# Packed-value products by 32-row parts of the array, into four banks, with new schedule constants

## The chip, the cores and the metric

The kernel runs on one core of a Trainium2 chip. The metric is the device time of one execution in microseconds. Before the change it is 819.77 us, the median of three runs (819.11 to 821.26). The engines are TensorE (PE in the profile; its weight loads are PEld), VectorE (DVE), ScalarE (ACT), GpSimd (POOL) and SyncE (SP), which issues the transfers.

## The reference

Eight batches, eight heads of width 64, 576 tokens. In each head 32 packing rows `p` attend over the keys and values and give 32 packed rows; then the 576 queries attend over the packed rows, which serve as keys and values both. The result, with the heads side by side (4608 tokens of 512), goes through an RMS norm and a gated MLP of inner width 1536.

```python
p_packed = sm_attn(p, k, v)              # 32 rows a head
out = sm_attn(q, p_packed, p_packed)
x = out.transpose(0, 2, 1, 3).reshape(B * S, H * D)
xn = x / rms * rms_g                      # rms = sqrt(mean(x*x) + 1e-6)
y = (silu(xn @ w_gate) * (xn @ w_val)) @ w_out
```

Outputs are float32, and the inputs `w_gate`, `w_val` and `w_out` are 64-bit numbers which the kernel turns into float32 itself.

## The kernel before

The 4608 tokens go in 12 units of 384 (three times 128 partitions). A unit is pure (its tokens are of one batch) or mixed (units 1, 4, 7 and 10: the first 64 partitions are of one batch, the other 64 of the next). Numbers are kept as a high and a low float16, so a product takes three matmuls: high by high, high by low, low by high. Units 0 and 1 compute scores in float32 instead (`early`).

Stage 1 (`stage1`, per batch) computes packing scores (L740, L749), their softmax, the transposes (L781) and the products with v (L795); the result for four heads lies on 128 partitions, 32 rows a head, in `pk`, one tile for each half of the heads. From it come `pbd` (packed rows as keys), `pg`, which `packed_weights` multiplies into the gate and value weights (L909, kept in `ring`), and `pav` (packed rows as values). The gated MLP's first product takes `ring` and the attention weights, so the attention output itself is only needed for its norm.

`attention` (per unit) multiplies the queries with `pbd` (L1048), makes a softmax and transposes the weights with a DMA (`aT`, L1088). Then it multiplies them with `pav`, squares the result and sums it: that is the attention output, and only its sum of squares for each token is used. `aT` holds on 128 partitions four heads of 32 weights each. So that one matmul serves four heads, `pav` is block-diagonal and 256 columns wide: `own` is a mask of ones in the block of each head and zeros elsewhere, and L870 multiplies it with `pk` (L875 and L877 split the result in high and low).

```python
nc.vector.scalar_tensor_tensor(pw, pks[g].unsqueeze(1).broadcast_to([P, 4, D]), sv, own, ALU.mult, ALU.mult)
```

For each third of a unit one bank (`pa`, of which there are two) takes 6 such matmuls (L1105), 12 in a mixed unit, and ScalarE squares it in place (L1110). After three of these GpSimd makes the norm (L1126 on), a one-row product (L1132) and a second transposing DMA give `aTu`. `mlp` then takes the big products: 24 groups of gate and value (L1199, four banks `pm`), activation and split (`gated`: L1233, L1236, L1241, L1247), and the output products with `w_out` (L1224).

At the start the weights come in as 1 MB pieces (`gv_piece` and `wo_piece`: L406, L411, L413), are scaled by L491, and `w_out` is summed (L523, L536, L540) and split (`wo_split`: L556, L559, L561, L567).

The order of all work on all engines is set by a planner in Python (`Plan.run`): each step is a generator that names an engine and an estimated cost, and the planner starts the step that could begin earliest, by due times (`RANK`), latencies (`LATENCY`), margins (`SLACK`, `CHOICE`) and free rooms (buffers). The estimates set only the order; on the chip each engine runs its list in order and waits on semaphores.

Of the kernel before, what the change touches and what calls it, by code (L numbers as in the profile page):

```python
# [211 lines left out]
def tile_packed_attention_then_swiglu(  # L212
# [68 lines left out]
    own = cpool.tile([P, 4, D], BF16, name="own")  # L281
    nc.gpsimd.memset(own, 0.0)
    for j in range(4):
        nc.gpsimd.memset(own[32 * j : 32 * j + 32, j, :], 1.0)

# [20 lines left out]
    rooms("pa", 2, [P, 512], F32, psum)  # L306
    rooms("psc", 1, [P, 2, 512], F32, psum)
# [410 lines left out]
    def stage1(b):  # L718
# [146 lines left out]
        for g in range(2):  # L865

            pw = yield Room("pw")
            hl = yield Room("pav")
# [1 line left out]
            nc.vector.scalar_tensor_tensor(  # L870
                pw, pks[g].unsqueeze(1).broadcast_to([P, 4, D]), sv, own, ALU.mult, ALU.mult
            )
# [148 lines left out]
    def attention(u):  # L1021
# [14 lines left out]
        yield PE, pe(64, 48) if early else len(parts(u)) * 36 * 0.03, None  # L1036
        for i in range(TPU):
            for b, r, o, n in parts(u):
                pbd = packs[b][3]
                for pi in range(4):  # L1040
                    if early:
# [4 lines left out]
                        continue  # L1046
                    for j, (lq, lp) in enumerate(((0, 0), (0, 1), (1, 0))):
                        nc.tensor.matmul(  # L1048
                            ps2[o : o + n, i, :, pi, :], qT[:, lq, i, pi, o : o + n], pbd[:, lp, pi, :, :],
                            start=(j == 0), stop=(j == 2),  # L1050
                        )
# [46 lines left out]
        for i in range(TPU):
            px = yield Room("pa")
            yield PE, pe(256, 6), t_a  # L1100
            for b, r, o, n in parts(u):
                pav = packs[b][2]
                for g in range(2):
                    for j, (la, lp) in enumerate(((0, 0), (0, 1), (1, 0))):
                        nc.tensor.matmul(  # L1105
                            px[o : o + n, 256 * g : 256 * g + 256], aT[:, i, la, g, o : o + n], pav[g][:, lp, :],
                            start=(j == 0), stop=(j == 2),
                        )
            yield ACT, act(512) + 0.2
            nc.scalar.activation(px, px, AF.Square, scale=2.0**-14, accum_out=ss[:, i : i + 1])  # L1110
            plan.give("pa", px)
# [223 lines left out]
```

## Time and profile before

| | |
|---|---|
| median of three runs | 819.77 us (819.11 to 821.26) |
| the profiled execution | 822.24 us, span 820.5 |
| TensorE busy | 762.2 us (93%), 6638 matmuls |
| VectorE busy | 496.5 us (61%) |
| ScalarE busy | 470.7 us (57%) |
| GpSimd busy | 98.0 us (12%) |
| granted TensorE clock, mean | 0.959 |
| L1105, products with packed values | 33.07 us busy, 288 matmuls |
| L1048, scores of units 2 to 11 | 14.41 us busy, 468 matmuls |

Busy time counts overlapping matmuls once, and the end of a matmul is modelled, so the length of a group is better read from the chain of waits, where each piece reaches to the start of the next. In rows of matmuls the shapes are rows x columns of the stationary weights, then output. An "x12" behind a row is the number of instructions merged in it.

### The profile page before, as it was taken

How to read it: one execution, taken by the hardware profiler on the slowest of the kernel's cores; microseconds unless marked ns; L12 is line 12 of the kernel's file. 1: busy time of each engine (PE TensorE's matmuls, PEld its weight loads, DVE VectorE, ACT ScalarE, POOL GpSimd, SP SyncE). 2: the span in 40 equal slices, each digit the busy share in tenths (PEclk: the TensorE clock that was granted, in tenths of full speed). 3: DMA queues.
4: the chain of work that ended last, by engine and by line, in shares of the span. 5: the costliest groups of instructions: out<-in, count | busy, mean ns of one | idle time of the engine just before them, and what ended most of it. 6: DMA issues, size and time to landing. Idle time of an engine off the chain costs nothing.

```text
span 820.5 us, 16153 instructions
## 1 busy us (share of the span) xinstructions
PE 762.2 (93%) x6638; PEld 445.2 (54%) x6638; DVE 496.5 (61%) x1001; ACT 470.7 (57%) x837; POOL 98.0 (12%) x149
## 2 busy tenths in 40 slices
PE   5686887989999999999979999999999999999998
PEld 4353453468555455477444556477455555576553
DVE  1797678387388367386748385566577465464341
ACT  2747887476468457467567457368566455272230
POOL 2556606100001000101010001000000001000000
PEclk9558797999999999999999999999999999999999
DMA  9991621426341940562627341725337212311001
GB/s 259 382 283 65 212 91 30 103 43 145 79 106 31 208 113 6 95 139 59 132 52 147 80 106 48 161 71 112 69 73 145 66 33 59 67 31 34 26 1 39
DMA packets 135497, 82.04 MB, mean 100 GB/s; under 512 B 98432, under 2 KB 123008, under 8 KB 135424
## 3 DMA queue, kind: packets, MB, share of 16 engines
q1 hardware_dynamic: 135424, 81.02, 41.3%
q8 instruction: 52, 0.85, 0.4%
q14 instruction: 21, 0.17, 0.1%
HBM read 47.97 MB, written 9.44 MB: 70 GB/s over the span
## 4 chain that ended last, share of the span: by engine, by line
PE 76%; DVE 9%; ACT 8%; DMA 3%; issue 2%; POOL 1%; SPq 1%; DVEq 0%; ACTq 0%; POOLq 0%
PE pm_0x L1224 9%; PE pm_1x L1224 9%; PE pm_3x L1199 8%; PE pm_2x L1224 7%; PE pm_1x L1199 7%; PE pm_2x L1199 7%; PE pm_3x L1224 7%; PE pm_0x L1199 7%; PE pm_0x L909 2%; DMA ring<-in_moe_w_gate_dram 2%; PE psc_0x L1048 2%; PE pa_0x L1105 2%; PE pa_1x L1105 2%; PE pm_2x L909 1%; DVE ring L365 1%
## 5 line engine op out<-in xcount | busy, mean ns | idle before, releaser
L1199 PEld LDWEIGHTS <-ring 128*128 128x128 f16 x2304 | 206.3, 98 | 112.4 <-issue 41.2
L1224 PEld LDWEIGHTS <-hall 128*128 128x128 f16 x1296 | 123.6, 98 | 154.9 <-issue 16.5
L1224 PE MATMUL pm_1x<-wo,hall 128*128 128x512 f16 x360 | 83.2, 381 | 5.6 <-POOL wo L567 3.1
L1224 PE MATMUL pm_0x<-wo,hall 128*128 128x512 f16 x360 | 82.4, 379 | 0.0
L1224 PE MATMUL pm_2x<-wo,hall 128*128 128x512 f16 x324 | 72.6, 379 | 0.0
L1241 ACT CAST hall<-t_1x 128x384 f16<-128x384 f32 x72 | 36.7, 510 | 43.4 <-DVE t_1x L1236 42.8
L1224 PE MATMUL pm_3x<-wo,hall 128*128 128x512 f16 x252 | 56.9, 379 | 0.0
L1199 PE MATMUL pm_3x<-aTu_1x,ring 128*128 128x192 f16 (+1 forms) x372 | 50.8, 281 | 1.6 <-ACT t_1x L1233 1.1
L1241 ACT CAST hall<-t_0x 128x384 f16<-128x384 f32 x72 | 36.6, 509 | 26.6 <-DVE t_0x L1236 25.9
L1247 DVE TENSOR_TENSOR hall<-t_1x,hall 128x384 f16<-128x384 f32 x72 | 40.0, 556 | 18.1 <-ACT hall L1241 16.7
L1247 DVE TENSOR_TENSOR hall<-t_0x,hall 128x384 f16<-128x384 f32 x72 | 41.1, 571 | 13.7 <-ACT hall L1241 13.4
L1199 PE MATMUL pm_3x<-aTu_0x,ring 128*128 128x384 f16 (+1 forms) x300 | 45.3, 294 | 0.4 <-ACT t_1x L1233 0.2
L1199 PE MATMUL pm_1x<-aTu_0x,ring 128*128 128x192 f16 (+1 forms) x306 | 42.4, 282 | 1.4 <-DVE tiny_30x L775 1.3
L1199 PE MATMUL pm_2x<-aTu_0x,ring 128*128 128x192 f16 (+1 forms) x306 | 42.4, 282 | 0.0
L1199 PE MATMUL pm_2x<-aTu_1x,ring 128*128 128x384 f16 (+1 forms) x246 | 38.1, 297 | 3.6 <-DVE ring L365 2.6
L1199 PE MATMUL pm_1x<-aTu_1x,ring 128*128 128x384 f16 (+1 forms) x276 | 40.1, 288 | 0.1
L1199 PE MATMUL pm_0x<-aTu_1x,ring 128*128 128x192 f16 (+1 forms) x258 | 38.4, 295 | 1.2 <-ACT t_1x L1233 1.1
L1199 PE MATMUL pm_0x<-aTu_0x,ring 128*128 128x384 f16 (+1 forms) x240 | 35.5, 290 | 0.0
L1105 PEld LDWEIGHTS <-aT_0x 128*128 128x128 f16 (+1 forms) x288 | 23.7, 104 | 9.4 <-issue 5.8
L1233 ACT ACT_TABLE_LOAD x15 | 19.2, 1283 | 7.4 <-PE pm_1x L1199 2.8
L363 ACT ACTIVATE ring<-pm_2x,pw_sc 128x512 f16<-128x512 f32 x27 | 18.4, 683 | 6.9 <-PE pm_3x L909 4.7
L365 DVE SCALAR_TENSOR_TENSOR ring<-pm_0x,pw_sc,ring 128x512 f16<-128x512 f32 x26 | 19.4, 745 | 4.4 <-ACT ring L363 3.9
(848 smaller groups left out, 1312.6 us busy)
## 6 DMA issues: line engine op xcount, KB each, us to landing
out_dram<-o_1x SPq DMA_DIRECT2D x18, 256.0 KB, 2.2
out_dram<-o_0x SPq DMA_DIRECT2D x18, 256.0 KB, 2.0
wo<-in_moe_w_gate_dram SPq DMA_DIRECT2D x3, 1024.0 KB, 15.3
wo<-in_moe_w_val_dram SPq DMA_DIRECT2D x3, 1024.0 KB, 13.7
ring<-in_moe_w_out_dram SPq DMA_DIRECT2D x3, 1024.0 KB, 6.0
hall<-in_moe_w_out_dram SPq DMA_DIRECT2D x3, 1024.0 KB, 5.4
big_0x<-in_k_dram SPq DMA_DIRECT2D x5, 576.0 KB, 6.9
big_2x<-in_k_dram SPq DMA_DIRECT2D x5, 576.0 KB, 6.2
```

Source lines behind the costliest of these rows:

```text
L363: nc.scalar.activation(hi, x, AF.Copy, scale=s)
L365: nc.vector.scalar_tensor_tensor(lo, x, s, hi, ALU.mult, ALU.subtract)
L909: nc.tensor.matmul(ps[e][32 * j : 32 * j + 32, :], pg[h, j, :], wgv[h, c, j, :, :].rearrange("p w f -> p (w f)"), start=True, stop=True,)
L1048: nc.tensor.matmul(ps2[o : o + n, i, :, pi, :], qT[:, lq, i, pi, o : o + n], pbd[:, lp, pi, :, :], start=(j == 0), stop=(j == 2),)
L1105: nc.tensor.matmul(px[o : o + n, 256 * g : 256 * g + 256], aT[:, i, la, g, o : o + n], pav[g][:, lp, :], start=(j == 0), stop=(j == 2),)
L1199: nc.tensor.matmul(psi[:, :, o : o + n], pw[:, g, lw, w, f * P : (f + 1) * P], aT[:, :, la, g, o : o + n], start=(j == 0), stop=(j == 5),)
L1224: nc.tensor.matmul(po, hall[:, ft, lh, ts], wo[:, ft, lw, :], start=(n == 0), stop=(n == 3 * NFT - 1))
L1233: nc.scalar.activation(t, pss[0][:, :UT], AF.Silu, scale=sc[:, c, 0:1])
L1241: nc.scalar.copy(hall[:, ft, 0, :], t)
L1247: nc.vector.tensor_tensor(hall[:, ft, 1, :], t, hall[:, ft, 0, :], ALU.subtract)
```

## The change

- `pav` is no longer block-diagonal. It keeps the 32 rows of each head where they lie on the partitions, 64 columns wide, and is split straight from `pk` by the helper `split` (in the profile its lines are those of L363 and L365). `own`, `pw` and L870 to L877 are gone.
- A matmul of the packed values now takes 32 rows of the array (one head, `tile_position=(32 * j, o)`) and 64 columns of output. The four heads j write into four different banks. A pure unit has 72 such matmuls (3 thirds x 2 halves x 3 terms x 4 heads) where it had 18, a mixed one 144 where it had 36, each with its own weight load.
- The four banks are one tile `quad`; its first two are the old `psc` and the other two the old `pa`. The block of a whole unit takes all four at once, then come the three squares, each over 128 columns of each bank, then the banks are given back.
- In the scores of a mixed unit (L1048) the two batches' matmuls alternate (they use different columns of the array), where before the first batch's twelve came ahead of the second's.
- `LATENCY`, `SLACK`, `CHOICE` and `RANK` get other values, and the two steps other estimated costs; with them the planner sets another order.

```diff
-LATENCY = {PE: 0.25, ACT: 0.16, EXP: 0.16, SILU: 0.16, DVE: 0.14, POOL: 0.1}
-SLACK = (0.3, 0.3)
-CHOICE = {"pe": 0.0, "act": 0.3, "dve": 0.3, "pool": 0.5, "sp": 0.3}
+LATENCY = {PE: 0.293, ACT: 0.16, EXP: 0.16, SILU: 0.16, DVE: 0.14, POOL: 0.1}
+SLACK = (0.306, 0.3)
+CHOICE = {'pe': 0.1, 'act': 0.335, 'dve': 0.324, 'pool': 0.378, 'sp': 0.437}
...
-    "scales": 0.1, "gated": 0.2, "pw_evict": 0.3, "store": 0.4, "attention": 0.5, "stage1": 0.6, "keys": 0.65, "v": 0.66,
-    "query": 0.7, "pw": 0.8, "g": 0.9, "w": 1.0, "wo": 1.5, "wo_split": 1.8,
+RANK = {"scales": 0.1, "gated": 0.44, "pw_evict": 0.3, "store": 0.4, "attention": 0.63, "stage1": 0.6, "keys": 0.67, "v": 0.66, "query": 0.79, "pw": 0.8, "g": 0.9, "w": 1.0, "wo": 1.5, "wo_split": 1.65}
...
-    rooms("pa", 2, [P, 512], F32, psum)
-    rooms("psc", 1, [P, 2, 512], F32, psum)
+    quad = psum.tile([P, 4, 512], F32, name="quad")
+    plan.rooms["psc"] = [(0.0, quad[:, 0:2])]
+    plan.rooms["pa"] = [(0.0, quad[:, 2]), (0.0, quad[:, 3])]
...
-            nc.vector.scalar_tensor_tensor(
-                pw, pks[g].unsqueeze(1).broadcast_to([P, 4, D]), sv, own, ALU.mult, ALU.mult
-            )
+            yield from split(hl[:, 0], hl[:, 1], pks[g], sv, D, t_s)
             plan.give("pk", pks[g])
-            yield ACT, act(256)
-            nc.scalar.copy(hl[:, 0], pw.rearrange("p h d -> p (h d)"))
-            yield DVE, dve(256) + 0.1
-            nc.vector.tensor_tensor(hl[:, 1], pw.rearrange("p h d -> p (h d)"), hl[:, 0], ALU.subtract)
...
-        yield PE, pe(64, 48) if early else len(parts(u)) * 36 * 0.03, None
+        yield PE, pe(64, 48) if early else 36 * 0.03 + 0.1 * len(parts(u)), None
         for i in range(TPU):
-            for b, r, o, n in parts(u):
-                pbd = packs[b][3]
-                for pi in range(4):
+            for pi in range(4):
...
-                    for j, (lq, lp) in enumerate(((0, 0), (0, 1), (1, 0))):
+                for j, (lq, lp) in enumerate(((0, 0), (0, 1), (1, 0))):
+                    for b, r, o, n in parts(u):
                         nc.tensor.matmul(
...
-        for i in range(TPU):
-            px = yield Room("pa")
-            yield PE, pe(256, 6), t_a
-            for b, r, o, n in parts(u):
-                pav = packs[b][2]
-                for g in range(2):
-                    for j, (la, lp) in enumerate(((0, 0), (0, 1), (1, 0))):
-                        nc.tensor.matmul(
-                            px[o : o + n, 256 * g : 256 * g + 256], aT[:, i, la, g, o : o + n], pav[g][:, lp, :],
-                            start=(j == 0), stop=(j == 2),
-                        )
-            yield ACT, act(512) + 0.2
-            nc.scalar.activation(px, px, AF.Square, scale=2.0**-14, accum_out=ss[:, i : i + 1])
-            plan.give("pa", px)
+        held = [("psc", (yield Room("psc")))]
+        for _ in range(2):
+            held.append(("pa", (yield Room("pa"))))
+        px = quad[:, :, : TPU * 2 * D].rearrange("s j (i g d) -> s j i g d", i=TPU, g=2)
+        yield PE, pe(D, 6 * TPU) + 0.4, t_a
+        for i in range(TPU):
+            for g in range(2):
+                for n3, (la, lp) in enumerate(((0, 0), (0, 1), (1, 0))):
+                    for j in range(4):
+                        h = slice(32 * j, 32 * j + 32)
+                        for b, r, o, n in parts(u):
+                            nc.tensor.matmul(
+                                px[o : o + n, j, i, g, :], aT[h, i, la, g, o : o + n], packs[b][2][g][h, lp, :],
+                                start=(n3 == 0), stop=(n3 == 2), tile_position=(32 * j, o),
+                            )
+        t = plan.now
+        for i in range(TPU):
+            yield ACT, act(512) + 0.2, t
+            x = px[:, :, i].rearrange("s j g d -> s j (g d)")
+            nc.scalar.activation(x, x, AF.Square, scale=2.0**-14, accum_out=ss[:, i : i + 1])
+        for name, room in held:
+            plan.give(name, room)
```

The order moves on every engine. Three places are shown; in the changed kernel the line numbers are smaller (L1099 is the old L1105, L1197 the old L1199, L898 the old L909, L793 the old L795, L747 the old L749).

First, TensorE in unit 4's big products, around the packed-value products of unit 5. Before, from stage 1's value products on (weight loads and equal rows in between are left out):

```order
L795 MATMUL pa_1x<-big_2x,a1T_0x 32x64 x24
...
L1199 MATMUL pm_3x<-aTu_0x,ring 128x3x64
...
L1105 MATMUL pa_0x<-pav_2x,aT_0x 128x256
...
L1105 MATMUL pa_0x<-pav_3x,aT_0x 128x256
...
L749 MATMUL psc_0x<-big_5x,pT_0x 32x288
...
L1105 MATMUL pa_1x<-pav_2x,aT_0x 128x256
...
L1132 MATMUL pa_1x<-ru_1x,onesb 128x3
```

And in the changed kernel:

```order
L793 MATMUL quad<-big_2x,a1T_0x 32x64 x24
...
L1197 MATMUL pm_2x<-aTu_0x,ring 128x3x64
...
L1099 MATMUL quad<-pav_2x,aT_0x 128x64
...
L1099 MATMUL quad<-pav_3x,aT_0x 128x64
...
L898 MATMUL pm_1x<-wgv,pg_1x 32x512
...
L747 MATMUL quad<-big_5x,pT_0x 32x288
...
L1130 MATMUL quad<-ru_1x,onesb 128x3
```

The three pieces, which lay apart and on both sides of stage 1's scores, are one block now, 24 big products behind stage 1's value products and, with a packing pair and 36 big products between, ahead of its next scores. The products of unit 4 itself stand, in the changed kernel, two packing pairs and 54 big products behind that unit's scores (before: one pair, 96 big products and 39 output products).

Second, SyncE's transfers at the start. Before:

```order
L578 DMA big_0x<-in_k_dram 96x4x384
L578 DMA big_2x<-in_k_dram 96x4x384
L601 DMA pf_0x<-in_p_dram 32x2x64 x4
L578 DMA big_1x<-in_v_dram 96x4x384
L970 DMA wgv<-in_q_dram 128x8x192
L376 DMA o_0x<-in_moe_rms_g_dram 128x512
L444 DMA ring<-in_moe_w_gate_dram 128x4x512
L578 DMA big_3x<-in_v_dram 96x4x384
L378 DMA gcol<-in_moe_rms_g_dram 128x4x1
L444 DMA ring<-in_moe_w_val_dram 128x4x512
```

And in the changed kernel:

```order
L576 DMA big_0x<-in_v_dram 96x4x384
L576 DMA big_2x<-in_v_dram 96x4x384
L576 DMA big_1x<-in_k_dram 96x4x384
L576 DMA big_3x<-in_k_dram 96x4x384
L599 DMA pf_0x<-in_p_dram 32x2x64 x4
L959 DMA wgv<-in_q_dram 128x8x192
L374 DMA o_0x<-in_moe_rms_g_dram 128x512
L442 DMA ring<-in_moe_w_gate_dram 128x4x512
L376 DMA gcol<-in_moe_rms_g_dram 128x4x1
L442 DMA ring<-in_moe_w_val_dram 128x4x512
```

Both halves of batch 0's v went ahead of its keys; from the second piece of the weights on the same bytes are ahead as before.

Third, ScalarE late in unit 0's gate products, from the last sum of w_out's squares (L523, now L521) to the first casts of the split (L561, now L559). Before:

```order
L523 ACTIVATE o_0x,wo_ss<-wo_83 128x1024
L786 COPY a1T_0x<-psc_0x 96x768
L1233 ACT_TABLE_LOAD
L1233 ACTIVATE t_0x<-pm_1x,usc_0x 128x384
L1233 ACTIVATE t_1x<-pm_2x,usc_0x 128x384
L556 ACTIVATE big_2x<-wo_83,wo_sc 128x1024
...
L556 ACTIVATE big_5x<-wo_83,wo_sc 128x1024
L999 ACTIVATE big_3x,tiny_46x<-big_0x 128x8x3x64
L833 ACTIVATE pts_0x<-pa_0x,tiny_50x 128x128
L561 CAST wo_83<-big_2x 128x2x512
```

And in the changed kernel:

```order
L521 ACTIVATE o_0x,wo_ss<-wo_77 128x1024
L1231 ACT_TABLE_LOAD
L1231 ACTIVATE t_1x<-pm_3x,usc_0x 128x384
L1231 ACTIVATE t_0x<-pm_2x,usc_0x 128x384
...
L554 ACTIVATE big_0x<-wo_77,wo_sc 128x1024
...
L831 ACTIVATE pts_0x<-quad,tiny_47x 128x128
L554 ACTIVATE big_4x<-wo_77,wo_sc 128x1024
...
L559 CAST wo_77<-big_0x 128x2x512
```

The sum came forward from behind ten of the unit's twelve activations to behind seven, the square of the next query (L999) and three of its splits (L363) fell behind the last cast, and the casts of `pav` (L875) became the narrow L363 of `split`. On TensorE the product L540, which closes the sum, stands behind 108 of unit 0's 144 gate products instead of all of them.

More of the change, by code (lines that the diff above doesn't have):

```diff
@@ L50, in pe @@
     return count * max(n / 2400 + 0.0025, 0.029)
+ACT_COST = (0.076, 0.87e-3)
+DVE_COST = (0.08, 1.04e-3)
 def act(n):
-    return 0.1 + 0.87e-3 * n
+    return ACT_COST[0] + ACT_COST[1] * n
 def dve(n):
-    return 0.08 + 1.04e-3 * n
+    return DVE_COST[0] + DVE_COST[1] * n
 def pool(n):
@@ L279, in tile_packed_attention_then_swiglu @@
     nc.gpsimd.memset(qk1, QK)
[L281 to L284, printed above, removed]
     wgv = cpool.tile([P, NFC, NKT, 2, 2 * P], F32, name="wgv")
@@ L322, in tile_packed_attention_then_swiglu @@
     rooms("pg", 2, [P, 4, NPK], F32)
-    rooms("pw", 1, [P, 4, D], F32)
-    rooms("pav", 4, [P, 2, 4 * D], F16)
+    rooms("pav", 4, [P, 2, D], F16)
     rooms("junk", 2, [P, D], BF16)
@@ L1035, in attention @@
         ps2 = psx.rearrange("s (i e j r) -> s i e j r", i=TPU, e=2, j=4)
-        yield PE, pe(64, 48) if early else len(parts(u)) * 36 * 0.03, None
+        yield PE, pe(64, 48) if early else 36 * 0.03 + 0.1 * len(parts(u)), None
         for i in range(TPU):
-            for b, r, o, n in parts(u):
-                pbd = packs[b][3]
-                for pi in range(4):
-                    if early:
+            for pi in range(4):
+                if early:
+                    for b, r, o, n in parts(u):
                         nc.tensor.matmul(
@@ L1045, in attention @@
                         )
-                        continue
-                    for j, (lq, lp) in enumerate(((0, 0), (0, 1), (1, 0))):
+                    continue
+                for j, (lq, lp) in enumerate(((0, 0), (0, 1), (1, 0))):
+                    for b, r, o, n in parts(u):
                         nc.tensor.matmul(
-                            ps2[o : o + n, i, :, pi, :], qT[:, lq, i, pi, o : o + n], pbd[:, lp, pi, :, :],
+                            ps2[o : o + n, i, :, pi, :], qT[:, lq, i, pi, o : o + n], packs[b][3][:, lp, pi, :, :],
                             start=(j == 0), stop=(j == 2),
@@ L1097, in attention @@
         t_x = []
[L1098 to L1111 removed]
+        held = [("psc", (yield Room("psc")))]
[3 more added lines that the diff above has]
+        yield PE, pe(D, 6 * TPU) + 0.4, t_a
+        for i in range(TPU):
+            for g in range(2):
+                for n3, (la, lp) in enumerate(((0, 0), (0, 1), (1, 0))):
+                    for j in range(4):
+                        h = slice(32 * j, 32 * j + 32)
+                        for b, r, o, n in parts(u):
+                            nc.tensor.matmul(
[7 more added lines that the diff above has]
+            nc.scalar.activation(x, x, AF.Square, scale=2.0**-14, accum_out=ss[:, i : i + 1])
             t_x.append(plan.now)
+        for name, room in held:
+            plan.give(name, room)
         plan.give("aT", aT)
```

5 lines of the change are left out of this document (removed).

## The prediction

> **What bounds the kernel now.** I read the page first (span, busy shares, the row of slices), then the busy time in five stretches, then the chain that ended last.
>
> ```profile
> span 820.5 us, 16153 instructions
> PE 762.2 (93%) x6638; PEld 445.2 (54%) x6638; DVE 496.5 (61%) x1001; ACT 470.7 (57%) x837; POOL 98.0 (12%) x149
> core 0: us, PE busy (x) PEld busy (x) DVE busy (x) ACT busy (x) POOL busy (x), PEclk, DMA share, GB/s
> 0.00:90.00 90.00, 58.70 (x523) 37.33 (x523) 57.68 (x111) 50.63 (x76) 47.90 (x65) 0.74 0.81 243
> 90.00:120.00 30.00, 29.18 (x280) 17.52 (x272) 22.01 (x45) 27.32 (x49) 6.16 (x9) 0.97 0.49 155
> 120.00:160.00 40.00, 30.35 (x209) 15.22 (x210) 27.39 (x48) 26.00 (x43) 15.98 (x12) 0.87 0.27 62
> 160.00:750.00 590.00, 577.53 (x5294) 341.72 (x5293) 370.80 (x769) 354.74 (x648) 27.92 (x64) 0.99 0.41 87
> PE 76%; DVE 9%; ACT 8%; DMA 3%; issue 2%; POOL 1%; SPq 1%; DVEq 0%; ACTq 0%; POOLq 0%
> ```
>
> From 160 to 750 us TensorE is busy for 577.5 of 590 us at a granted clock of 0.99; VectorE has 371 us of work there (63%), ScalarE 355 (60%). After 750 us only products are left. So whatever leaves TensorE's queue after 160 us shortens the run almost one for one, until the 12.5 us of idle time grow. Before 160 us it is different: the DMA share is 0.81 up to 90 us, ScalarE has 27.3 of 30 us from 90 to 120 us, and TensorE idles 9.7 us from 120 to 160 us. The profiled execution took 822.24 us (1.7 outside its span) and the median of the runs shown is 819.77; I make the sum against the former and take 2.5 us off for the latter.
>
> **Products with packed values, as they are.** From the chain in order of time, one piece for a pure unit (one batch), then for a mixed one (two batches), with the score products L1048 of both kinds:
>
> ```profile
> 190.05 0.66 PE pa_1x L1105 x6
> 331.40 1.02 PE pa_0x L1105 x12
> 333.82 1.02 PE pa_1x L1105 x12
> 168.00 1.05 PE psc_0x L1048 x36
> 302.88 1.90 PE psc_0x L1048 x72
> 304.77 1.08 PE pm_1x L1199 x6
> 307.95 0.97 PE pm_1x L1199 x6
> 357.26 1.10 PE pm_2x L1199 x12
> 90.28 1.73 PE pm_3x L1199 x6
> ```
>
> Each unit has three pieces: 1.98 us in a pure unit, 3.06 in a mixed one. Seven pure units (2, 3, 5, 6, 8, 9, 11) and four mixed ones (1, 4, 7, 10) run after 150 us, 26.1 us in all. Unit 0 lies before 90 us, where TensorE has room, and I count it as nothing; if that room were gone it would be worth the 1.1 us that a pure unit saves below. The rows of L1199 give the pace of the big products around (six in 0.97 to 1.08 us in a pure unit, twelve in 1.10 in a mixed one) and the first of them, at 90.3 us.
>
> **What they become.** 72 matmuls of 32 rows x 64 columns in a pure unit and 144 in a mixed one, each with its own weight load. The arithmetic in rows of the array is a quarter; the time depends on whether four row parts (times two column parts in a mixed unit) run at once. No such matmul is in the trace. Its nearest relatives are the packing products (64 rows x 32 columns, eight parts, timeline of TensorE) and the stage-1 products (four column parts, first and last start of 48):
>
> ```profile
> 301.79 0.61 PE L909 MATMUL pm_0x<-wgv,pg_1x 64*32 64x512 f32 x1
> ...
> 301.83 0.61 PE L909 MATMUL pm_2x<-wgv,pg_1x 64*32 64x512 f32 x1
> 302.24 0.59 PE L909 MATMUL pm_0x<-wgv,pg_1x 64*32 64x512 f32 x1
> ...
> 302.81 0.38 PE L1048 MATMUL psc_0x<-pbd,big_1x 128*64 128x64 f16 x6
> L795 PE MATMUL pa_0x<-big_5x,a1T_0x x48: 219/219/243, 118.3 to 118.9; 96*32 96x64 f32 x48
> ```
>
> Eight packing products start within 0.04 to 0.05 us, some 6.5 ns apart, and all eight of the next round 0.45 us later: parts with different rows and columns do run together. Two rounds take 1.02 us up to the next line, of which 0.90 is streaming, so a block of another tiling costs about 0.12 us for going in and out. The 48 stage-1 products follow each other at 0.6/47 = 13 ns, the fastest pace that is shown over a long run.
>
> - Low end: 18 rounds. A round takes the larger of one 64-column product (1.05/36 = 29 ns) and its issue at 6.5 ns each (26 ns for four, 52 for eight). Pure 18 x 29 + 0.12 us = 0.65 us, mixed 18 x 52 + 0.12 us = 1.06 us.
> - High end, still overlapping: 13 ns for each instruction. Pure 72 x 13 + 0.12 us = 1.06 us, mixed 144 x 13 + 0.12 us = 1.99 us.
> - No overlap at all is a rival below.
>
> The packing products are nearer in kind (row parts), the stage-1 products in length of the run, so I take the middle: 0.86 and 1.53 us. Saved: 7 x 1.12 = 7.8 and 4 x 1.53 = 6.1 us; ends 6.4 to 9.3 and 4.3 to 8.0.
>
> **Score products of mixed units.** The two batches write different column halves of the array; in turn instead of one after the other they should pair, so that 72 cost what 36 of a pure unit cost, 1.05 us, instead of 1.90. Three units (4, 7, 10): 2.6 us; nothing if column parts don't pair, which the 13 ns above speak against. The fp32 products of unit 1 are interleaved too, in a stretch where TensorE idles, so I count nothing. Sum on TensorE: 16.5 us.
>
> **Around the block.** Four banks are held at once, and the three squares follow the whole block instead of a third of it.
>
> ```profile
> L1110 ACT ACTIVATE pa_0x<-pa_0x x19: 577/582/607, 67.8 to 729.3; 128x512 f32<-128x512 f32 x19
> L1110 ACT ACTIVATION_READ_ACCUMULATOR pa_0x<-pa_0x x19: 181/194/202, 68.3 to 729.8; 128x1 f32 x19
> PE pa_0x L1105 <- ACT pa_0x L1110: 0.2, 1, 0.2
> 476.00 1.97 PE L1048 MATMUL psc_0x<-pbd,big_1x 128*64 128x64 f16 x72
> ...
> 486.71 1.44 SPq L1088 DMA_TRANSPOSE aT_0x<-hl_0x  x1
> DMA to landing us min/median/max: 3.6/3.7/4.4
> ```
>
> The squares are as many and as long: 3 x (0.58 + 0.19) = 2.3 us a unit, on an engine with 40% to spare. From the end of the scores (302.88 + 1.90 gives their length; here 476.0 + 1.9 = 477.9) to the landing of aT (486.7 + 3.7 = 490.4) it is 12.5 us. In the new order unit 4 has two packing pairs and 54 products of L1199 between scores and block, 2 x 1.02 + 9 x 0.97 = 10.8 us: 1.7 us short. The other units have 12 us or more by the same count. I put down 2 us lost, between 0 and 4. Behind the waiting matmul stands the whole of TensorE.
>
> **Packed values.** Each batch loses two wide VectorE products and their casts:
>
> ```profile
> L870 DVE SCALAR_TENSOR_TENSOR pw_0x<-pk_2x,tiny_50x,own x1: 2350/2350/2350, 131.4 to 131.4; 128x256 f32<-128x256 f32 x1
> L870 DVE SCALAR_TENSOR_TENSOR pw_0x<-pk_0x,tiny_80x,own x1: 484/484/484, 225.3 to 225.3; 128x256 f32<-128x256 f32 x1
> ```
>
> Later, at 0.48 us, that hides under TensorE's 98% and is worth nothing (if VectorE became the bound, about 1 us a batch). At 131 us, where TensorE waits, it counts in the next part.
>
> **Start.** Here the constants move things.
>
> ```profile
> GB/s 259 382 283 65 212 91 30 103 43 145 79 106 31 208 113 6 95 139 59 132 52 147 80 106 48 161 71 112 69 73 145 66 33 59 67 31 34 26 1 39
> big_0x<-in_k_dram SPq DMA_DIRECT2D x5, 576.0 KB, 6.9
> PE pm_1x L1224 <- POOL wo L567: 3.1, 2, 1.6
> PE pm_1x L1224 <- ACT wo L561: 2.5, 1, 2.5
> PE pa_1x L819 <- ACT junk_1x L807: 3.0, 1, 3.0
> L999 ACT ACTIVATE big_5x<-big_2x 128x1536 bf16<-128x1536 f32 x2 | 3.0, 1481 | 1.6 <-DMA big_2x<-in_q_dram 1.6
> L363 ACT ACTIVATE ring<-pm_2x,pw_sc 128x512 f16<-128x512 f32 x27 | 18.4, 683 | 6.9 <-PE pm_3x L909 4.7 <-PE pm_0x L909 1.9 <-PE pm_1x L909 0.3
> ```
>
> Against: SP now loads both halves of v ahead of k. At the 382 GB/s of the second slice a half of 576 KB is 1.5 us, so k, the first products behind it and SP's queue start up to 3 us later; the weights move back by 1.5 us at first and not at all from the second piece on, since the same bytes are then ahead. For: ScalarE reaches the last cast of w_out (L561) with one L999 (1.5 us) and three L363 of the next query (3 x 0.68) less ahead of it and one ring eviction more, some 2.9 us less, and the sum of w_out's squares stands 36 products of L1199 earlier on TensorE. The 8.6 us of waits quoted are what this can reach. I take 2 us gained, between 6 gained and 4 lost.
>
> **Sum.** 16.5 - 2 + 2 = 16.5 us: 822.24 becomes 805.7 for a profiled run, and 819.77 becomes 803.3 for the median, about 803. With all ends together, 19.9 + 6 = 25.9 gained gives 794, and 13.3 - 4 - 4 = 5.3 gained gives 814.5.
>
> **Rivals.**
>
> 1. The parts don't overlap: one instruction in a row costs what L1048 shows, 29 ns at 128 columns and 1.90/72 = 26.4 ns at 64. Pure 72 x 29.2 + 0.12 us = 2.22 us (+0.24), mixed 144 x 26.4 + 0.12 us = 3.92 us (+0.86), the scores stay: 1.7 + 3.4 us lost, start and late aT cancel, 819.8 + 5.1 = 825. For it: in L1048 every 64-column product costs its whole 26 to 29 ns. Against it: L909's 6.5 ns. [...] Chance 0.08.
>
> 2. Only column parts overlap. Pure as in 1 (+1.7 us), mixed 144 x 13.2 + 0.12 us = 2.02 us (4 x 1.04 saved), scores 2.6 saved: 5.1 us gained, 815. L795 shows column parts alone; row parts are shown with 64 rows only. Chance 0.12.
>
> 3. The late k and the new order of w_out's work cost 6 us instead of gaining 2: 803.3 + 8 = 811. ScalarE's 27.3 of 30 us speak for it, the equal amount of DMA against it. Chance 0.12.
>
> 4. Slower: the block needs all four banks free, and holds them until ScalarE has squared them. In units 5 and 8 stage 1's value products end 24 products (2.2 us) ahead of the block and its next scores come 36 products and a packing pair (4.3 us) behind it; if VectorE's read or the 2.3 us of squares queue behind the activation of the gate, TensorE stops. It decides from 16.5/11 = 1.5 us a unit on; at 2.5 us a unit the time is 803.3 + 27.5 = 831. For it: the old kernel could use three rooms in turn. Against: its wait for a bank is 0.2 us in the whole run, and ScalarE and VectorE idle for 40%. Chance 0.08.
>
> **Chances and range.** Forecast 0.6, rivals 0.08, 0.12, 0.12, 0.08. A measurement of this kernel tells about 0.3% (2.5 us) from no change, so faster is below 817.3: the forecast, rivals 2 and 3, 0.84. Rival 1 lies at the edge of the other side; I give 0.06 to no change and 0.10 to slower. The range goes from 793 to 816: the forecast's ends and rivals 2 and 3.
>
> **What would show it.** In the new timeline, four starts of the block's matmuls within some 30 ns, a pure block of 0.65 to 1.06 us, a mixed one of 1.06 to 1.99, mixed scores near 1.05. Waits for aT at unit 4 of 1 to 2 us. TensorE idle from 160 us on no more than some 14 us. Scores or stage-1 products waiting for a square (L1110's successor) over 1.5 us a unit would make rival 4; a pure block above 2 us makes rival 1 or 2; a first product of L1199 later than 93 us makes rival 3 (it now starts at 90.3).

## The result, and the profile after

The changed kernel takes 797.96 us (median; 796.5 to 799.99), the kernel before 820.0 us in the same comparison (819.11 to 821.26): a ratio of 0.973, with an interval from 0.971 to 0.976. The profiled executions took 796.5 and 822.24 us, spans of 794.5 and 820.5.

First the chain of waits of the changed kernel (start, length, engine, group, count): a pure block, then scores and block of a mixed unit, then the block of the next mixed unit.

```profile
178.07 0.68 PE quad L1099 x72
...
293.81 1.26 PE quad L1037 x72
309.15 1.30 PE quad L1099 x144
...
475.85 1.43 PE quad L1099 x144
```

A pure block takes 0.68 us (0.69 and 0.75 in two units) where three pieces took 1.98, a mixed one 1.30 to 1.43 (1.49 in unit 1) where they took 3.06, and the mixed scores 1.26 where they took 1.90.

Next the stretch that the sum was about. It is cut here at the first big product of unit 1 and at the last matmul, so that it holds the same products before and after, except for unit 2's pure scores (1.05 us), which the changed kernel has already done. The columns are length, then busy time and count of TensorE, weight loads, VectorE, ScalarE and GpSimd, then the granted clock, the DMA share and GB/s. Before, then after:

```profile
166.80:816.50 649.70, 637.19 (x5599) 371.50 (x5597) 385.71 (x791) 363.00 (x666) 27.31 (x62) 0.99 0.37 81
```

```profile
166.10:790.80 624.70, 617.59 (x6265) 356.53 (x6263) 375.86 (x774) 364.37 (x668) 27.90 (x62) 1.00 0.38 84
```

TensorE is busy 19.6 us less and idle 7.1 us instead of 12.5. The clock rises from 0.99 to 1.00, and that small step matters. Here is the kernel before around its wait in unit 1, from the timeline and then in stretches of 1 us:

```profile
183.04 1.46 PE L1199 MATMUL pm_2x<-aTu_1x,ring 128*128 128x192 f16 x12 [2.64 <-DVE ring L365]
184.56 2.08 PE L1199 MATMUL pm_0x<-aTu_1x,ring 128*128 128x192 f16 x12
```

```profile
182.00:183.00 1.00, 0.00 (x0) 0.00 (x0) 1.00 (x3) 1.00 (x2) 0.00 (x0) 1.00 0.00 0
183.00:184.00 1.00, 0.96 (x11) 0.94 (x11) 1.00 (x2) 0.98 (x2) 0.00 (x0) 0.87 0.00 0
184.00:185.00 1.00, 0.94 (x8) 0.68 (x6) 1.00 (x2) 0.99 (x2) 0.00 (x0) 0.50 0.06 16
185.00:186.00 1.00, 1.00 (x9) 0.92 (x7) 0.96 (x2) 0.73 (x3) 0.00 (x0) 0.50 0.96 182
186.00:187.00 1.00, 1.00 (x9) 0.92 (x7) 0.25 (x1) 0.51 (x1) 0.00 (x0) 0.50 1.11 198
187.00:188.00 1.00, 1.00 (x18) 0.83 (x24) 0.89 (x3) 0.53 (x2) 0.00 (x0) 0.93 0.99 152
```

After a wait of 2.64 us the clock is granted at 0.50 for some 3.4 us, and the twelve products that start at 184.56 take 1.88 us up to the next twelve, instead of 1.10. That is 3.4 x 0.5 = 1.7 us lost beyond the wait. The kernel before has two such drops from 160 us on (the other behind two waits close together, of 2.8 and 1.1 us), the changed kernel none. The waits of that time, before and after (engine, group, what it waited for, us in total, times, longest):

```profile
PE pa_0x L1132 <- POOL ru_0x L1128: 2.8, 1, 2.8
PE pm_2x L1199 <- DVE ring L365: 2.6, 1, 2.6
PE pm_3x L1199 <- ACT t_1x L1233: 1.3, 2, 1.1
PE pm_1x L1199 <- DVE tiny_30x L775: 1.3, 1, 1.3
```

```profile
PE pm_3x L1197 <- DVE ring L363: 1.7, 1, 1.7
PE pm_3x L1197 <- ACT t_1x L1231: 1.0, 1, 1.0
PE quad L747 <- ACT quad L1107: 0.7, 1, 0.7
...
PE quad L1099 <- DMA aT_0x<-hl_0x: 0.3, 1, 0.3
```

So the 26.0 us between the spans come apart as follows: idle time 12.5 - 7.1 = 5.4; two clock drops 3.4; work on TensorE 15.1 (the difference of the busy time, 19.6, less the drops, less the 1.05 us of scores that moved ahead of the cut); the lead at the cut 0.7 + 1.05 = 1.8; and 0.3 behind the last matmul. I had forecast 15.0 us of work behind the cut (16.5 with unit 1's block, which lies ahead of it), and nothing for the idle time and the clock. Added up from the pieces of the chain, the blocks and scores behind the cut save 16 us; where the other 0.9 us of the busy time went, no run shows.

### The profile page after: what moved, and what is told of

Its sections match the earlier page's. It is cut to its first block, busy times and chain, and to the rows that moved or that the text cites. A ratio compares the mean times of both kernels' runs of the same rounds, so it can differ in the third digit from the quotient of the medians.

```text
span 794.5 us, 17852 instructions
## 1 busy us (share of the span) xinstructions
PE 737.0 (93%) x7502; PEld 425.1 (54%) x7502; DVE 483.9 (61%) x985; ACT 472.2 (59%) x839; POOL 101.4 (13%) x144
## 4 chain that ended last, share of the span: by engine, by line
PE 78%; ACT 7%; DVE 6%; DMA 5%; SPq 2%; issue 2%; POOL 1%; ACTq 0%; DVEq 0%; POOLq 0%
PE pm_2x L1222 11%; PE pm_1x L1222 10%; PE pm_2x L1197 8%; PE pm_1x L1197 8%; PE pm_0x L1222 8%; PE pm_3x L1197 7%; PE pm_0x L1197 7%; PE pm_3x L1222 6%; DMA hall<-in_moe_w_gate_dram 2%; PE pm_3x L898 2%; SPq L442 2%; PE quad L1037 1%; DMA big_3x<-in_k_dram 1%; PE pm_0x L898 1%; PE quad L793 1%
## 5 line engine op out<-in xcount | busy, mean ns | idle before, releaser
L1197 PEld LDWEIGHTS <-ring 128*128 128x128 f16 x2304 | 205.7, 98 | 107.0 <-issue 35.9
L1222 PE MATMUL pm_2x<-wo,hall 128*128 128x512 f16 x396 | 90.1, 379 | 0.0
L1239 ACT CAST hall<-t_1x 128x384 f16<-128x384 f32 x72 | 36.8, 510 | 34.9 <-DVE t_1x L1234 34.3
L1245 DVE TENSOR_TENSOR hall<-t_1x,hall 128x384 f16<-128x384 f32 x72 | 41.7, 579 | 17.2 <-ACT hall L1239 14.8
L1245 DVE TENSOR_TENSOR hall<-t_0x,hall 128x384 f16<-128x384 f32 x72 | 41.6, 578 | 14.9 <-ACT hall L1239 14.6
L1222 PE MATMUL pm_3x<-wo,hall 128*128 128x512 f16 x216 | 49.2, 383 | 0.0
L1197 PE MATMUL pm_2x<-aTu_0x,ring 128*128 128x192 f16 (+1 forms) x324 | 45.6, 285 | 1.0 <-DVE ring L363 0.6
L1197 PE MATMUL pm_1x<-aTu_1x,ring 128*128 128x192 f16 (+1 forms) x324 | 45.8, 285 | 0.2 <-ACT t_0x L1231 0.2
L1197 PE MATMUL pm_3x<-aTu_1x,ring 128*128 128x192 f16 (+1 forms) x288 | 41.2, 286 | 3.1 <-DVE ring L363 1.7
L1197 PE MATMUL pm_1x<-aTu_0x,ring 128*128 128x192 f16 (+1 forms) x312 | 43.5, 283 | 0.2 <-ACT t_0x L1231 0.2
L1197 PE MATMUL pm_2x<-aTu_1x,ring 128*128 128x192 f16 (+1 forms) x288 | 41.3, 286 | 0.9 <-ACT hall L1239 0.7
L1197 PE MATMUL pm_0x<-aTu_0x,ring 128*128 128x384 f16 (+1 forms) x270 | 40.2, 291 | 0.7 <-ACT t_1x L1231 0.3
L1197 PE MATMUL pm_3x<-aTu_0x,ring 128*128 128x384 f16 (+1 forms) x246 | 37.6, 296 | 0.6 <-ACT t_1x L1231 0.5
L1197 PE MATMUL pm_0x<-aTu_1x,ring 128*128 128x384 f16 (+1 forms) x252 | 36.6, 288 | 0.0
L363 DVE SCALAR_TENSOR_TENSOR ring<-pm_3x,pw_sc,ring 128x512 f16<-128x512 f32 x31 | 23.1, 745 | 9.1 <-ACT ring L361 9.0
L361 ACT ACTIVATE ring<-pm_3x,pw_sc 128x512 f16<-128x512 f32 x31 | 21.1, 682 | 7.3 <-PE pm_0x L898 5.7
L1107 ACT ACTIVATE quad<-quad 128x512 f32<-128x512 f32 x36 | 21.1, 587 | 6.7 <-PE quad L1099 6.2
L363 DVE SCALAR_TENSOR_TENSOR ring<-pm_0x,pw_sc,ring 128x512 f16<-128x512 f32 x27 | 20.1, 746 | 7.8 <-ACT ring L361 7.4
## 6 DMA issues: line engine op xcount, KB each, us to landing
wo<-in_moe_w_val_dram SPq DMA_DIRECT2D x3, 1024.0 KB, 10.8
```

Of the source, the lines that this page charges most:

```text
L361: nc.scalar.activation(hi, x, AF.Copy, scale=s)
L363: nc.vector.scalar_tensor_tensor(lo, x, s, hi, ALU.mult, ALU.subtract)
L1107: nc.scalar.activation(x, x, AF.Square, scale=2.0**-14, accum_out=ss[:, i : i + 1])
L1197: nc.tensor.matmul(psi[:, :, o : o + n], pw[:, g, lw, w, f * P : (f + 1) * P], aT[:, :, la, g, o : o + n], start=(j == 0), stop=(j == 5),)
L1222: nc.tensor.matmul(po, hall[:, ft, lh, ts], wo[:, ft, lw, :], start=(n == 0), stop=(n == 3 * NFT - 1))
L1239: nc.scalar.copy(hall[:, ft, 0, :], t)
```

## Experiments: what a block costs

All comparisons are with the kernel before, timed on the same chip (820.4 to 820.7 us).

**Heads in turn.** The head j becomes the outermost loop, so that neighbouring matmuls of a batch use the same 32 rows. The order of everything else stays.

```diff
+        for j in range(4):
+            h = slice(32 * j, 32 * j + 32)
-        for i in range(TPU):
-            for g in range(2):
-                for n3, (la, lp) in enumerate(((0, 0), (0, 1), (1, 0))):
-                    for j in range(4):
-                        h = slice(32 * j, 32 * j + 32)
+            for i in range(TPU):
+                for g in range(2):
+                    for n3, (la, lp) in enumerate(((0, 0), (0, 1), (1, 0))):
```

> The changed kernel with the four heads outermost in the block: the same 72 or 144 matmuls, banks and squares, but 18 in a row use the same 32 rows of the array. Theory A (the gain is that neighbours use different row parts and run at once): a pure block takes 72 x 29 ns = 2.1 us instead of 0.68, a mixed one about half of 144 x 29 ns = 2.1 instead of 1.3 to 1.5; 7 x 1.4 + 4 x 0.7 = 12.6 us more, 811. Rival (short matmuls with a quarter of the rows are quick in any order): blocks as they are, 798.

Measured: 809.09 us, ratio 0.985 (0.982 to 0.987), 11.1 us above the changed kernel. From its chain, and its stretch from unit 1 on:

```profile
180.68 1.90 PE quad L1099 x72
...
314.53 2.10 PE quad L1099 x141
```

```profile
168.70:803.70 635.00, 628.32 (x6265) 367.52 (x6263) 375.72 (x774) 365.56 (x668) 27.99 (x62) 1.00 0.37 83
```

72 matmuls through the same rows take 1.90 us, 26.4 ns each; spread over four row parts they take 0.68, 9.4 ns each. So the row parts do run at once, and that is where the gain of a pure block lies. In a mixed unit the two column parts alone bring it to 2.10/144 = 14.6 ns. Whether the 26.4 ns are a cost of each matmul or the time of its columns, no run here shows: the big products take 0.97 us for six times 384 columns, 0.42 ns a column, so that 64 columns streamed one matmul after the other would take 27 ns as well (an estimate from these rows). The 9.4 ns show that across row parts this time is not paid by each matmul in turn.

This run also measures what TensorE's time is worth when the order is fixed: 7 x 1.22 us in pure blocks and 0.80 + 0.67 + 0.80 in mixed ones make 10.8 us, the busy time grows by 10.7 and the stretch by 10.3. One for one.

**Half the columns.** Each of the block's matmuls writes 32 columns, and the squares read only these; half of each head's attention output is left out of the norm.

```diff
-    px[o : o + n, j, i, g, :], aT[h, i, la, g, o : o + n], packs[b][2][g][h, lp, :],
+    px[o : o + n, j, i, g, : D // 2], aT[h, i, la, g, o : o + n], packs[b][2][g][h, lp, : D // 2],
...
-            x = px[:, :, i].rearrange("s j g d -> s j (g d)")
+            x = px[:, :, i, :, : D // 2]
```

> The block's matmuls write 32 columns of output where they wrote 64, and the squares read those alone: half of each head's attention output is left out of the norm. The order and the number of instructions stay. Theory A (a block is limited by issue, about 9 ns for a matmul with its weight load): a pure block stays at 0.65 to 0.70 us. Rival B (limited by the columns streamed through each row part): a pure block of 0.35 to 0.45 us. Total within 2 us of 798 by A, 3 to 5 us less by B; the squares are half as long (on ScalarE, with room).

Measured: 795.86 us in a single run, 2.1 us below the changed kernel's median but 0.6 below its profiled execution. The timeline of the same pure block, in the changed kernel and here:

```profile
178.01 0.27 PE L1099 MATMUL quad<-pav_2x,aT_0x 32*128 32x64 f16 x12
...
178.47 0.28 PE L1099 MATMUL quad<-pav_3x,aT_0x 32*128 32x64 f16 x12
178.68 0.61 PE L898 MATMUL pm_0x<-wgv,pg_1x 64*32 64x512 f32 x1
```

```profile
179.06 0.24 PE L1099 MATMUL quad<-pav_2x,aT_0x 32*128 32x32 f16 x12
...
179.51 0.27 PE L1099 MATMUL quad<-pav_3x,aT_0x 32*128 32x32 f16 x12
179.71 0.61 PE L898 MATMUL pm_0x<-wgv,pg_1x 64*32 64x512 f32 x1
```

The block shrinks from 0.67 to 0.65 us although half the columns are gone; 60 of the 72 matmuls start within 0.46 and 0.45 us. So here not the streaming but the number of matmuls, some 8 ns for one with its weight load, sets the length; whether the matmul or its load sets the pace, no run separates. One rival comes close in a pure block: a fixed 26.4 ns in each row part, shared by four parts, would give 6.6 ns. The mixed block speaks against it: there eight parts run, and a matmul still takes 1.30/144 = 9.0 ns.

**Scores apart.** In mixed units the two batches' scores follow each other again, as before the change.

```diff
-            for pi in range(4):
...
-                for j, (lq, lp) in enumerate(((0, 0), (0, 1), (1, 0))):
-                    for b, r, o, n in parts(u):
+            for b, r, o, n in parts(u):
+                for pi in range(4):
+                    for j, (lq, lp) in enumerate(((0, 0), (0, 1), (1, 0))):
```

> The changed kernel, but in the scores of mixed units the first batch's twelve matmuls come ahead of the second's again; everything else stands in the same order. Theory A: each of the three mixed score groups goes from 1.26 back to 1.90 us on a TensorE without room, 798 + 1.9 = 800. Rival: the time is taken up by a later wait, 798.

Measured: 800.07 us, ratio 0.975 (0.974 to 0.977), 2.1 us above the changed kernel. Its chain, the same wait in its timeline as the changed kernel's 1.7 us on `ring`, and the clock behind it:

```profile
293.47 1.90 PE quad L1038 x72
```

```profile
303.23 1.41 PE L1198 MATMUL pm_3x<-aTu_1x,ring 128*128 128x384 f16 x6 [2.02 <-DVE ring L363]
```

```profile
304.00:305.00 1.00, 1.00 (x5) 0.46 (x3) 1.00 (x2) 0.99 (x2) 0.00 (x0) 0.50 0.00 0
```

The scores are back at 1.90 us, 3 x 0.64 = 1.9 us in all, close to the difference of the medians. The profiled execution shows something beside it: the wait is 0.36 us longer, and a clock drop of 1.7 us follows it. Its span is 2.8 us longer than the changed kernel's, with a start of unit 1 that is 0.7 us earlier. How much of the medians' difference is scores and how much is clock is therefore not shown.

## Experiments: what the order costs

The planner's numbers were part of the change: LATENCY, SLACK, CHOICE, RANK, and its estimate of a ScalarE step (0.1 us + 0.87 ns an element before, 0.076 us + 0.87 ns now). The estimate stands in the planner's cost functions, and the account of the change above leaves it out; the first two runs left it as the kernel they started from had it. In all these kernels the instructions of the products are those of the kernel named; only the numbers, and with them the order, differ. In the expectations "theory A" means what each text says there, not one theory throughout.

**The changed kernel with the old four, and the kernel before with the new four.**

```diff
-LATENCY = {PE: 0.293, ...}; SLACK = (0.306, 0.3); CHOICE = {'pe': 0.1, ...}; RANK = {..., "gated": 0.44, ...}
+LATENCY = {PE: 0.25, ...};  SLACK = (0.3, 0.3);   CHOICE = {"pe": 0.0, ...}; RANK = {..., "gated": 0.2, ...}
```

> The changed kernel with the old LATENCY, SLACK, CHOICE and RANK: new products, order made by the old constants. Theory A (the gain is TensorE's time in the two groups of products, 15.5 us in the packed-value products and 2.0 in the mixed scores, and the other 4.5 us of the 22 are waits that the new order avoids): 800.5 to 804, about 802.5, the blocks still 0.68 us (pure) and 1.3 to 1.5 (mixed). Rival B (most of the gain comes from the order that the constants make): 810 or more. If the constants are worth nothing: 798.

> The kernel before with the new LATENCY, SLACK, CHOICE and RANK: old products, order made by the new constants. Theory A: 4.5 us of waits avoided, 813 to 818, about 815.5. Rival B: 808 or less. Rival C (the constants fit the new products alone): 820 or more.

Measured: 815.86 us (ratio 0.995, 0.993 to 0.996) and 835.75 us (1.018, 1.016 to 1.020). My theory, that the constants are worth a few us by themselves (800.5 to 804 and 813 to 818), fell on both sides: the new products alone gained 4.6 us, the new four constants alone lost 15.3, both together gained 22. Since the estimate had stayed behind, the next two runs moved all five.

**All five old with the new products, all five new with the old products, and the estimate alone, in each kernel.**

```diff
-ACT_COST = (0.076, 0.87e-3)
+ACT_COST = (0.1, 0.87e-3)
```

This is the estimate going back in the changed kernel; in the kernel before it goes the other way, and the two runs with all five have the four of above with it.

> The new products with every planner constant of before; the estimated cost of a ScalarE step (0.1 us + 0.87 ns an element, where the change and the earlier run with old constants had 0.076) goes back too. Theory A (new products in an order that is not fitted to them keep their saving on TensorE and give most of it back as waits): within 4 us of that earlier run's 815.9, so 812 to 820, with TensorE idle 10 us or more from 160 to 750 us beyond the 7.1 us of the changed kernel. Rival B (the mixture of old constants with the new ScalarE cost was what failed; a consistent old set carries the products' 16 us): 806 or less.

> The old products with every new planner constant, the ScalarE cost of 0.076 us among them. Theory A (the new constants fit the new products alone): 825 to 840, near the 835.8 without that cost. Rival B (only the missing ScalarE cost made that run slow, the new constants are better by themselves): 815 or less.

> The changed kernel with one number back: the planner's estimate of a ScalarE step, 0.1 instead of 0.076 us. Theory A (any number reorders the whole list, and an order is good or bad as a whole): 803 to 816, the time lost is TensorE's idle time from 160 us on, the blocks stay at 0.68 and 1.31 to 1.50 us. Rival B (the order is worth little, time follows TensorE's work): within 2 us of 798.

```diff
-    return 0.1 + 0.87e-3 * n
+    return 0.076 + 0.87e-3 * n
```

> The kernel before with the planner's estimate of a ScalarE step at 0.076 instead of 0.1 us, nothing else. Theory A (any number reorders the whole list; the old order was one of the better ones for the old products): 820 to 836. Rival B (this estimate is the better one, whatever the products): 817 or less.

Measured: 812.98 us (ratio 0.991, 0.990 to 0.993), 821.11 (1.001, 0.999 to 1.002), 801.49 (0.977, 0.975 to 0.978) and 828.66 (1.010, 1.007 to 1.012). So with all five moved the new constants do nothing for the old products, and "they fit the new products alone and harm the old ones" (825 to 840) fell too, as did its rival (815 or less). The estimate alone in the changed kernel came out between theory A (803 to 816) and its rival (within 2 us of 798); the other two lie in theory A's ranges. One estimate, changed by 0.024 us, costs 3.5 us in the changed kernel and 8 us in the one before.

**RANK alone, and LATENCY, SLACK and CHOICE alone, back in the changed kernel.**

```diff
-RANK = {..., "gated": 0.44, ..., "attention": 0.63, ..., "keys": 0.67, ..., "query": 0.79, ..., "wo_split": 1.65}
+RANK = {..., "gated": 0.2, ..., "attention": 0.5, ..., "keys": 0.65, ..., "query": 0.7, ..., "wo_split": 1.8}
```

> The changed kernel with the old RANK (the due times) alone; the other constants stay new. Theory A (each set of numbers is another whole order, none of the constants has a price of its own): 801 to 813, and TensorE's waits from 160 us on rise by about what the time rises. Rival B (RANK carries the fit): 810 or more, near the 813.0 with all constants old, and then the run with the other constants old is within 2 us of 798.

```diff
-LATENCY = {PE: 0.293, ...}; SLACK = (0.306, 0.3); CHOICE = {'pe': 0.1, 'act': 0.335, 'dve': 0.324, 'pool': 0.378, 'sp': 0.437}
+LATENCY = {PE: 0.25, ...};  SLACK = (0.3, 0.3);   CHOICE = {"pe": 0.0, "act": 0.3, "dve": 0.3, "pool": 0.5, "sp": 0.3}
```

> The changed kernel with the old LATENCY, SLACK and CHOICE; RANK stays new. Theory A: 801 to 813, as for the old RANK alone. Rival B (RANK carries the fit): within 2 us of 798. Rival C (these three carry it): 810 or more.

Measured: 808.5 us (ratio 0.984, 0.983 to 0.986) and 816.36 (0.995, 0.993 to 0.996). RANK back costs 10.5 us, the three others 18.4, all five together only 15.0. RANK lies in theory A's range, though TensorE's idle time rises by 4.2 us only (table below); the three others lie above that range, where rival C had them. The parts don't add up; no constant has a price of its own.

**k first.** The first load of v gets a later due time, so that SP loads k and p ahead of v, as before the change.

```diff
-    plan.add(load_v(0), due("v", 0))
+    plan.add(load_v(0), due("v", 0) + 2.0)
```

> The changed kernel with the first load of v due later, so that k and p go first at the start, as before the change. TensorE's first wait, for p, falls from 13.8 to about 9.4 us. Theory A (the start up to 90 us is set by the weights' transfers and by ScalarE, and the early products have room): the first big product still starts at 84 to 86 us, and the time is 798 to 806, as this number too reorders the list. Rival B (the 4.4 us at the start are on the path): 793 to 796.

Measured: 800.27 us, ratio 0.975 (0.974 to 0.977), 2.3 us slower. From its waits:

```profile
PE pm_0x L610 <- DMA pf_0x<-in_p_dram: 8.7, 1, 8.7
PE quad L793 <- DMA big_4x<-in_v_dram: 6.0, 1, 6.0
```

TensorE's first wait falls from 13.8 to 8.7 us, and 6.0 us of wait for v come in its place. The first big product starts at 88.2 us instead of 84.8. So the time lies in theory A's range, the start (84 to 86 us) does not. From unit 1 on the run is the changed kernel's again (624.6 and 624.7 us).

**All orders in one table.** The stretch from unit 1's first big product to the last matmul, in us, ordered by time. "Lost to clock" is the sum over stretches of 0.25 us of TensorE's busy time x (1 - granted clock); "idle" is length less busy time, so a drop during a wait counts once, as idle time.

| kernel | time | unit 1 starts | busy | of it lost to clock | idle |
|---|---|---|---|---|---|
| old products, own constants (before) | 820.6 | 166.8 | 637.2 | 3.4 | 12.5 |
| old products, all five new | 821.1 | 167.7 | 635.0 | 3.0 | 12.4 |
| old products, estimate new | 828.7 | 169.2 | 636.2 | 3.2 | 15.2 |
| old products, four new | 835.8 | 169.8 | 637.7 | 3.4 | 23.8 |
| new products, own constants (after) | 798.0 | 166.1 | 617.6 | 0 | 7.1 |
| new products, k first | 800.3 | 169.6 | 617.7 | 0 | 6.9 |
| new products, estimate old | 801.5 | 163.9 | 617.9 | 0 | 14.9 |
| new products, RANK old | 808.5 | 171.8 | 621.7 | 2.9 | 11.3 |
| new products, all five old | 813.0 | 161.7 | 626.8 | 7.8 | 18.6 |
| new products, four old | 815.9 | 166.3 | 625.1 | 4.6 | 18.7 |
| new products, three old | 816.4 | 166.8 | 622.5 | 3.2 | 21.6 |

Busy time without the clock's loss is 632.1 to 634.3 us with the old products and 617.6 to 620.5 with the new ones. Counting unit 2's scores alike (they lie ahead of the cut in all but the kernel before and the runs with all five and with three old), the means are 634.1 and 619.4, and the orders of either kernel lie within 3 us: the products are worth 14.6 us of TensorE's work in all eleven orders. What an order adds in this stretch is 7 to 24 us of idle time and 0 to 8 us of clock, and that decides what a single swap seems to show. The four sets of constants that were run with both products give 7.6, 12.8, 34.3 and 23.1 us for the products, 19 in the mean.

The clearest case is the new products with all five old constants, so the plain exchange of the products under the old numbers. Its stretch, the longest waits in it, and the clock around the first of them:

```profile
161.70:807.10 645.40, 626.84 (x6301) 362.77 (x6299) 376.65 (x778) 362.49 (x667) 28.03 (x62) 0.98 0.37 82
```

```profile
PE pm_0x L1200 <- DMA aTu_0x<-hl_0x: 4.3, 1, 4.3
PE pm_0x L1200 <- DVE ring L366: 3.2, 2, 2.6
PE pm_2x L1200 <- DVE ring L366: 3.0, 2, 2.8
PE quad L700 <- ACT big_4x L694: 2.6, 1, 2.6
```

```profile
343.00:344.00 1.00, 0.00 (x0) 0.00 (x0) 0.00 (x0) 0.00 (x0) 0.00 (x0) 0.63 1.13 212
344.00:345.00 1.00, 0.00 (x0) 0.00 (x0) 0.00 (x0) 0.00 (x0) 0.00 (x0) 0.50 1.12 300
...
349.00:350.00 1.00, 1.00 (x11) 0.92 (x9) 0.78 (x1) 0.00 (x0) 0.00 (x0) 0.50 0.98 209
```

From 343 to 345 us no engine computes: the products of a unit wait 4.3 us for the transposing DMA of `aTu`, and run at a granted clock of 0.50 until 350 us. Against the kernel before, that order gains 5.1 us at the start and 637.2 - 3.4 - (626.8 - 7.8) = 14.8 us of work, and gives back 6.1 us in idle time and 4.4 us in clock: 9.4 of the 9.7 us between the spans.

What stays open: why one order has these waits and another not. The waits fall on different products each time (`ring`, `t_1x`, `aTu`, `aT`, the sums on GpSimd), and no run here says which numbers would be best; the changed kernel is the quickest of all that were run.

## Why the prediction was right, and where it was wrong

The time (803 forecast, 798 measured) lies in the range, and the main term is right: 15.0 us were forecast for the work from unit 1 on (16.5 less the block of unit 1, which lies ahead of it), 15.1 measured. The terms, one by one:

- **Pure block**, forecast 0.86 us, measured 0.68 (up to 0.75), near the low end (0.65). The mechanism was right, four row parts at once; the size was off because I took the middle between a pace of 6.5 and one of 13 ns, and it was some 8 ns. Some 7 x 1.30 = 9.1 us instead of 7.8.
- **Mixed block**, forecast 1.53, measured 1.30 to 1.49. My low end took the pace of instructions for the bound, and it is, at 9.0 ns each instead of the 6.5 I had put: 144 matmuls cost about twice what 72 do, so the second column half brings nothing beyond the four row parts.
- **Mixed scores**, forecast 1.05 (a full overlap of the two column halves), measured 1.26, 1.9 us saved instead of 2.6.
- **Late `aT`**, 2 us forecast, 0.3 us of wait measured from 160 us on. The failing step is "two packing pairs and 54 products, 10.8 us": a count of work leaves out the waits between, on the banks of the packing products and on `ring`. In unit 4 the scores end at 293.81 + 1.26 = 295.1 and the block starts at 309.15, 14.1 us later, a wait of 1.7 us for `ring` among them.
- **Start**, 2 us forecast, and here the forecast was too high. Ahead of the cut it had 3.5 us in all, with the 1.5 us of unit 1's block; measured are 1.8, the lead of 0.7 and the 1.05 us of scores that moved ahead. Unit 1's block itself is 1.57 us shorter (3.06 to 1.49), and how much of this its stretch kept, with TensorE idle for 8.8 of the 40 us from 120 to 160 us, is not shown. The first big product did start 5.4 us earlier (84.84 instead of 90.28), but most of that was lost before unit 1: from 90 to 120 us TensorE idles 4.6 us (last row below) where it idled 0.8. Part of the argument was wrong too: k did come later (13.8 us of first wait instead of 9.4), but moving it ahead again only made v late, and cost 2.3 us.

```profile
PE pm_0x L610 <- DMA pf_0x<-in_p_dram: 13.8, 1, 13.8
PE quad L932 <- DVE e_0x L1064: 7.5, 2, 4.1
```

```profile
90.00:120.00 30.00, 25.45 (x241) 14.91 (x239) 20.56 (x43) 25.29 (x47) 5.37 (x5) 0.89 0.32 105
```

- **The term that was missing.** I costed the new order from 160 us on at nothing, and it brought 5.4 us of idle time and 3.4 us of clock. The sentence "whatever leaves TensorE's queue shortens the run almost one for one, until the 12.5 us of idle time grow" is right for a fixed order (heads in turn: 10.7 us for 10.3), and its second half is what an exchange of the products alone ran into. I treated the order's effect as something of the start only. I also read the 0.99 of the clock as full speed; it stood for two drops, 3.4 us.

The rivals: 1 and 2 (no overlap, column parts only) fall by the 0.68 us and by heads in turn, whose 1.90 us is what a pure block takes where the row parts don't overlap. Rival 3 (late k costs 6 us) falls: the first big product starts at 84.84 us. Rival 4 (four banks at once) falls: the only wait for a square is the 0.7 us of L747 shown above.

```profile
84.84 1.14 PE L1197 MATMUL pm_0x<-aTu_0x,ring 128*128 128x384 f16 x6 [0.21 <-DVE ring L363]
```

So the total is right by a sound main term, and by a range wide enough for misses of both signs: the work behind the cut came near the forecast, 1.7 us of what was forecast ahead of it did not come, 2 us were charged for a wait that did not come either, and 8.8 us of idle time and clock, which had no place in the sum, were won. That the time lies 5 us below the forecast, and not some 10 above it, was luck with the order: the same products under other constants took up to 816.4 us, just outside the range. The median moved less (22.0 us) than the two profiled executions (25.7), since the profiled one of the changed kernel was its quickest run and that of the kernel before was longer than its timed ones.

## What to carry to other kernels

Here small products on different row parts of the array overlapped, and then cost by their number (8 to 9 ns for one with its weight load) and not by their columns (0.67 us a pure block at 64, 0.65 at 32): count them. Four row parts brought the 26.4 ns of a matmul down to 9.4, two column parts alone to 14.6, and both together to 9.0. Where a planner sets the order, price an edit in two sums, the work it removes from the bound engine (here the same within 3 us in seven orders of one kernel and in four of the other) and the idle time and clock that its order has; the second can be as large as the first, so an edit tried in one order alone can seem worth 8 or 34 us. When TensorE is at 98%, read its granted clock to the second decimal and look for the few waits behind it (here 0.99 instead of 1.00 was two drops, 3.4 us).

## What the runs showed of the hardware that I had not expected

- **Drops of the clock came with short pauses.** Several pauses of about 2 to 4 us in an otherwise full TensorE came with 3.4 us at a granted clock of 0.50, or with twice that. In the kernel before it was 3.41 us behind a pause of 2.64 us, and again behind one of 2.80 us with 1.10 us beside it; with RANK old 6.8 us from within a pause of 1.95 us on, with all five old 6.8 us from within one of 4.29 us on. Single pauses of 1.66 us (the changed kernel's longest from unit 1 on) and 1.88 us (old products, all five new) had none. It is not the length alone: 2.02 us came with a drop in the run with the scores apart, and 2.02 and 2.80 us did not in the run with the estimate alone, whose timeline and clock behind the longer pause are these:

```profile
417.02 1.14 PE L1197 MATMUL pm_0x<-aTu_1x,ring 128*128 128x384 f16 x6 [2.80 <-DVE ring L363]
```

```profile
416.00:417.00 1.00, 0.00 (x0) 0.00 (x0) 1.00 (x3) 0.76 (x2) 0.00 (x0) 1.00 0.00 0
417.00:418.00 1.00, 0.98 (x7) 0.58 (x7) 1.00 (x2) 0.98 (x2) 0.00 (x0) 1.00 0.00 0
```

  What decides whether a pause has a drop, no run here shows.
- **The first matmuls of a mixed block came faster than the rest.** In unit 1's block the first 32 starts lie between 149.75 and 149.89 us, 4 to 5 ns apart; after a pause of 0.1 us the others follow 8 to 9 ns apart. The mixed blocks of units 4 and 7 show the same (32 starts in 0.14 us, then 0.1 us of pause); the pure block of unit 2 does not, it goes at some 8 ns from its first twelve on (60 starts in 0.46 us). Why, no run shows.

```profile
149.75 0.21 PE L1099 MATMUL quad<-pav_0x,aT_0x 32*64 32x64 f16 x1
149.75 0.21 PE L1099 MATMUL quad<-pav_2x,aT_0x 32*64 32x64 f16 x1
149.76 0.21 PE L1099 MATMUL quad<-pav_0x,aT_0x 32*64 32x64 f16 x1
```

- **Two column halves of 128 rows paired only in part**: 72 scores in 1.26 us, where 36 of full width take 1.05.
